# Early blocks of a routed expert layer: a second block's tokens chosen by 0/1 matrices, token lists read in another order, three subtractions on another engine

## The chip, the cores and the metric

The kernel runs on one core of a Trainium2 chip. The metric is the device time of one execution in microseconds, from the runs listed below. A profiled execution records every instruction of the five engines: TensorE (PE in the profile: matmuls and transposes), VectorE (DVE), ScalarE (ACT), GpSimd (POOL) and SyncE (SP, which here only starts DMAs and reads small numbers into its registers). Each engine takes its own instructions strictly in order; an instruction starts when the semaphores that it names have been raised by the engines or DMAs it depends on.

## The reference, cut to what matters

The program computes three layers one after the other: an attention with a feature map, a mixture of 8 experts weighted by a Sinkhorn table ("MoE1"), and a mixture of 8 experts in which every token goes to one expert only ("MoE2"). The change lies at the seam of the second and the third:

```
logits = xn @ en.T / tau                  # 2304 tokens, 8 experts
expert_idx = argmax(logits, axis=1)
gate_w = softmax(logits)[token, expert_idx]
for e in range(8):
    mask = expert_idx == e
    h = max(x[mask] @ w1[e], 0)           # 512 -> 1024
    out[mask] = gate_w[mask] * (h @ w2[e])  # 1024 -> 512
```

All of it is in fp32. Products on TensorE are made of three matmuls on high and low parts (high x high, low x high, high x low), so weights and activations are split into a rounded high part (ScalarE) and the rest (VectorE).

## The kernel before, in words

**MoE1** goes over pairs (expert group n = 0..15, third of the tokens bi), 768 tokens each. At the end of the list stand the thirds 0, 1, 2 of the last group. When a third is done, its 6 tiles of 128 tokens are final rows of x, and are routed while the next third is being multiplied: `route_a` (transposes, row norms, rows to DRAM `x2d`, L896 on), `route_l` (logits), `route_b`/`route_o` (argmax as a 0/1 row), `route_c` (running counts by matmul), `route_s`/`route_d`/`route_w` (softmax weight and slot number of each token), and `route_i` (L988): GpSimd writes (token number, gate weight) of each token by an indirect DMA to its slot in one of the four DRAM tables `ids[0..3]` (tile number modulo 4). A slot is expert x 2304 + rank, so each expert's list lies packed.

**MoE2** goes over 22 static blocks of 128 tokens (`second(0, 22)`). The first 6 (`NEARLY`) hold only tokens of the first two thirds (`NF` = 12 tiles), so they can begin before the last third is routed; the others come from all tokens, after `other_blocks` has made their table. For each block:

- `load_regs` (SP) reads the block's offset, expert and "new expert" flag from the table `meta`; `load_ids` (L1108, SP) reads the block's piece of each of the four tables, four DMAs into `idr`. These wait for every scatter written ahead of them in the program.
- `gather` adds the four pieces (GpSimd for the first blocks, L1115 and L1116), casts the token numbers (L1123), and fetches the rows by an indirect DMA into `xgs` (L1125).
- `tx` (L1191) transposes the rows, and splits them into `xth` (ScalarE) and `xtl` (VectorE). `p1` is 24 matmuls of 128x512 (L1209 to L1211), `relu` (L1219) writes `hr`, `th_` (L1224 to L1228) transposes and splits it into `hTh` and `hTl`, `p2` is 24 matmuls (L1242 to L1244), scaled by the gate weight on ScalarE (`y`, L1249) and scattered to the output (L1250).
- `wcond` (L1157, SP) loads a quarter of the next block's W1 or W2 into `rw`, on the condition that the expert changes; `wsplit` makes the high part (`s1h`, `s2h`: ScalarE, L1182) and the low part (`s1l`, `s2l`: VectorE, L1183). A buffer of `rw` is loaded again when both have read it; the load's semaphore is raised also when the condition is false.

**The order** is written out by hand. `tail` is a table of (tick, function); ticks 0 to 39 lie in the second but last third of MoE1's work, 40 and above in the last one, whose plain part `p2_plain` (ticks 54 to 69) is six 128x384 matmuls to a tick. What follows, up to block 2, is the straight list in `second` under `if i0 == 0`. A function emits its instructions on all its engines at its place, and each engine's queue gets them in that order.

Block 0 is fetched otherwise: `gather_first` compares, for each of 12 tiles, the slot numbers less the block's offset with the row 0..127 (VectorE, L1141), and multiplies the twelve 0/1 matrices so made with the token numbers (12 matmuls of two columns, L1146). This gives its token numbers without `ids`. It is a generator of 8 steps; each step from the second on makes two compares. `load_ids(0)` and `gather(0)` then serve only the gate weight `gt[0]`, and `load_ids(1)`/`gather(1)` give block 1's rows.

Of the kernel before, what the change touches and what calls it, by code (L numbers as in the profile page):

```python
# [44 lines left out]
def build(tc, a, out):  # L45
# [836 lines left out]
    def batch(t0):  # L882
        if t0 not in rt:
            if t0 == TPB:
                pieces = [live["h3"].tile([P, 2 * TH], F32, tag="r" + q_, name=f"rows{t0}{q_}").unsqueeze(1)[:, :, 0:DM] for q_ in "abcd"]
                pieces += [raw().unsqueeze(1)[:, :, 0:DM] for _ in range(2)]
            else:
                pieces = [live["h3"].tile([P, 2, DM], F32, tag=f"hT{k + 2}", name=f"rows{t0}_{k}") for k in range(TPB // 2)]
# [55 lines left out]
    def route_c(t0):  # L944
        r = rt[t0]
        n, oh = r["n"], r["oh"]
        r["pr"] = psum("B" if t0 == TPB else "C", [P, 6, E])
# [95 lines left out]
    def first_blocks():  # L1043
# [19 lines left out]
        V.scalar_tensor_tensor(out=live["slots"][:, NF:NF + 1], in0=ei[:, 0:1], scalar=float(REG), in1=ri[:, 0:1], op0=ALU.mult, op1=ALU.add)  # L1063
# [37 lines left out]
    xgs = []  # L1101
# [8 lines left out]
    def gather(i):  # L1110
        ig = c0.tile([P, 2], F32, tag="gt", bufs=5, name=f"ig{i}")
        r = idr.pop(i)
        eng = G if i < NEARLY else V
        if i < NEARLY:
# [12 lines left out]
    def gather_first():  # L1127
# [19 lines left out]
        ig = live["slots"][:, NF + 1:NF + 2]  # L1147
        V.tensor_reduce(out=ig, in_=ps, axis=AX.X, op=ALU.add)
        idt[0] = c0.tile([P, 1], I32, tag="idt", bufs=5, name="idt0")
        V.tensor_copy(idt[0], ig)  # L1150
        xg[0] = xgs[0][:, 0, :]
        G.indirect_dma_start(out=xg[0], out_offset=None, in_=x2d[0:NF * P, :], in_offset=bass.IndirectOffsetOnAxis(idt[0][:, :1], 0))
# [24 lines left out]
    def wsplit(i, which, c):  # L1177
# [5 lines left out]
        V.tensor_tensor(out=lo, in0=r, in1=f32(hi), op=ALU.subtract)  # L1183
# [86 lines left out]
    def first_w1(i, cs):  # L1270
        for c in cs:
            wsplit(i, 1, c)
            wcond(i + 1, 1, c)

    def first_w2(i, cs):
        for c in cs:
            wsplit(i, 2, c)
# [97 lines left out]
    tail = route_steps(0, (1, 2, 4, 6, 8, 10), (1, 2, 3, 4, 5, 6), b=8, o=9, p=11, c=11, d=13, s=20, w=21, i=(22, 23, 24, 25, 26, 27))  # L1375
    tail += [(k, partial(route_l, TPB, i + 3 * (j // 4), (j % 4,))) for j, k in enumerate((19, 19, 21, 23, 25, 27, 29, 41)) for i in range(3)]
    tail += route_steps(6, (24, 26, 28, 41, 41, 42), (), p=42, b=41, o=41, c=42, d=42, s=56, w=57, i=(58, 58, 59, 60, 61, 62))
    tail += [(k, partial(next, rf, None)) for k in (43, 44, 46, 47, 62)]
    tail += [(k, partial(next, gf, None)) for k in (23, 49, 50, 51, 52, 53, 54, 56)]
    tail += [(48, partial(load_regs, 0)), (56, partial(load_regs, 1))]  # L1380
# [3 lines left out]
    tail += [(63, partial(load_ids, 1)), (63, partial(load_ids, 0)), (67, partial(gather, 1)), (67, partial(gather, 0)), (67, partial(load_ids, 2)), (68, partial(load_ids, 3))]  # L1384
# [61 lines left out]
    def second(i0, i1):  # L1446
        def w1_next(i, cs, hook=no):
            for c in cs:
                wsplit(i + 1, 1, c)
                hook()  # L1450
# [12 lines left out]
        if i0 == 0:  # L1463
            t0 = NA
            p1(0)
            gather(2)
            first_w1(1, (0, 1))
            first_w2(0, (3,))
            relu(0)
            first_w1(1, (2, 3))  # L1470
            load_ids(4)
# [10 lines left out]
            route_p(t0)  # L1482
            route_b(t0)
            route_o(t0)
            first_w1(2, (0,))
# [143 lines left out]
```

## Time and profile before

| | us |
|---|---|
| runs | 1898.66, 1898.28, 4289.9 |
| median | 1898.66 |
| the profiled execution | 1898.09 |
| its span, first to last instruction | 1896.2 |
| TensorE busy in it | 1878.8 (99%) |
| VectorE, ScalarE, GpSimd busy | 1284.2, 861.6, 968.5 |

All times inside the trace count from the start of the span. The last third of MoE1 ends at about 1610; block 0 of MoE2 begins there, and from block 2 on a block takes about 12.4 us. A row of a timeline gives start, duration, engine, line, operation, tiles and shape; in square brackets the idle time ahead of it and what ended that. `xN` folds N like instructions that follow each other.

### The profile page before, as it was taken

What the parts mean: (1) busy time and instruction counts of PE and PEld (TensorE: products, weight loads), DVE (VectorE), ACT (ScalarE), POOL (GpSimd) and SP (SyncE); (2) the same over time, 40 slices, a digit from 0 to 9 for tenths busy, and PEclk for the clock granted to TensorE, in tenths of its full rate; (3) what the DMA queues carried; (4) which work ended last, traced back from release to release, by engine and by line L of the source; (5) the groups of instructions that cost most, each with busy time, mean ns of one, the idle gap of its engine ahead of it and who ended that gap; (6) DMA issues with size and microseconds to landing.
All of it is one profiled execution on the core that took longest, in us unless ns stands there. A gap on an engine that the chain in (4) does not pass through costs nothing.

```text
span 1896.2 us, 34764 instructions
## 1 busy us (share of the span) xinstructions
PE 1878.8 (99%) x13649; PEld 1795.6 (95%) x13649; DVE 1284.2 (68%) x1667; ACT 861.6 (45%) x1258; POOL 968.5 (51%) x687
## 2 busy tenths in 40 slices
PE   9999999999999999999999999999999999999998
PEld 8999999999999999999999999999999998788886
DVE  7775676665756657567566575665656647899995
ACT  5674342433333333424243333333342324889885
POOL 0241377746556564747474655656474733522211
PEclk9999999999999999999999999999999999999999
DMA  5474544536372736354453637272635353263960
GB/s 169 153 277 184 216 153 152 178 125 213 103 244 90 252 86 224 114 189 157 147 178 125 212 103 245 79 263 83 228 114 189 117 181 123 63 224 101 339 207 33
DMA packets 125161, 314.47 MB, mean 166 GB/s; under 512 B 23336, under 2 KB 72248, under 8 KB 124994
## 3 DMA queue, kind: packets, MB, share of 16 engines
q1 hardware_dynamic: 120898, 301.69, 47.2%
q0 software_dynamic: 4096, 10.51, 1.6%
q8 instruction: 110, 1.80, 0.4%
q14 instruction: 57, 0.47, 0.1%
HBM read 335.29 MB, written 32.44 MB: 194 GB/s over the span
## 4 chain that ended last, share of the span: by engine, by line
PE 74%; POOL 14%; issue 6%; DVE 2%; DMA 2%; ACT 1%; POOLq 0%; SPq 0%; DVEq 0%; ACTq 0%
PE Q L414 16%; PE Q L415 15%; PE Q L413 15%; POOL w1S L333 3%; POOL hB L461 3%; POOL hT L461 3%; POOL w1A L333 2%; PE psR L146 2%; PE psA L1210 2%; PE psA L1209 2%; PE psA L1211 2%; PE psD L1244 2%; PE psD L1243 2%; PE psD L1242 2%; PE psD L203 2%
## 5 line engine op out<-in xcount | busy, mean ns | idle before, releaser
L477 DVE TENSOR_TENSOR acca<-acca,Q 128x768 f32<-128x768 f32 x196 | 181.4, 949 | 134.5 <-PE Q L415 134.5
L461 POOL TENSOR_TENSOR hB<-rb,hB 128x768 fp32r<-128x768 f32 x42 | 77.7, 1850 | 181.8 <-ACT hB L458 181.8
L413 PE MATMUL Q<-hT,w2S 128*128 128x384 f32 x504 | 169.9, 337 | 0.1
L415 PE MATMUL Q<-hT,w2S 128*128 128x384 f32 x504 | 168.5, 334 | 0.0
L414 PE MATMUL Q<-hT,w2S 128*128 128x384 f32 x504 | 168.4, 334 | 0.0
L415 PE MATMUL Q<-xT,w1S 128*128 128x384 f32 x504 | 168.3, 334 | 0.0
L413 PE MATMUL Q<-xT,w1S 128*128 128x384 f32 x504 | 168.3, 334 | 0.0
L414 PE MATMUL Q<-xT,w1S 128*128 128x384 f32 x504 | 168.3, 334 | 0.0
L477 DVE TENSOR_TENSOR accb<-accb,Q 128x768 f32<-128x768 f32 x98 | 90.7, 949 | 70.7 <-PE Q L415 70.7
L473 DVE TENSOR_TENSOR Q<-Q,ra 128x768 f32<-128x768 f32 x42 | 40.6, 966 | 132.1 <-PE Q L415 127.6
L333 POOL TENSOR_TENSOR w1A<-raw,w1A 128x512 fp32r<-128x512 f32 x48 | 62.7, 1307 | 131.0 <-ACT w1A L332 131.0
L482 ACT COPY ra<-Q 128x768 f32<-128x768 f32 x42 | 33.7, 801 | 188.0 <-PE Q L415 166.5
L415 PE MATMUL Q<-hB,w2A 128*128 128x384 f32 x338 | 113.0, 334 | 0.0
L413 PE MATMUL Q<-hB,w2A 128*128 128x384 f32 x338 | 112.9, 334 | 0.0
L414 PE MATMUL Q<-hB,w2A 128*128 128x384 f32 x338 | 112.9, 334 | 0.0
L461 POOL TENSOR_TENSOR hT<-ra,hT 128x768 fp32r<-128x768 f32 x42 | 77.5, 1844 | 69.2 <-ACT hT L458 69.2
L413 PE MATMUL Q<-xB,w1A 128*128 128x384 f32 x336 | 112.2, 334 | 0.0
L414 PE MATMUL Q<-xB,w1A 128*128 128x384 f32 x336 | 112.2, 334 | 0.0
L415 PE MATMUL Q<-xB,w1A 128*128 128x384 f32 x336 | 112.2, 334 | 0.0
L1183 DVE TENSOR_TENSOR s1l<-rw,s1h 128x1024 fp32r<-128x1024 f32 x88 | 102.5, 1218 | 4.0 <-ACT s1h L1182 2.4
L473 DVE TENSOR_TENSOR Q<-Q,rc 128x768 f32<-128x768 f32 x42 | 40.6, 966 | 91.6 <-PE Q L415 91.6
L461 POOL TENSOR_TENSOR hT<-rd,hT 128x768 fp32r<-128x768 f32 x42 | 77.7, 1851 | 47.4 <-ACT hT L458 47.4
(477 smaller groups left out, 6124.0 us busy)
## 6 DMA issues: line engine op xcount, KB each, us to landing
xT<-xpd SPq DMA_DIRECT2D x120, 768.0 KB
rw<-in_moe_w SPq DMA_DIRECT2D x176, 512.0 KB
xB<-xpd SPq DMA_DIRECT2D x90, 768.0 KB
raw<-in_moe_w SPq DMA_DIRECT2D x34, 512.0 KB
gate<-gd SPq DMA_DIRECT2D x45, 384.0 KB
rx<-in_moe_w SPq DMA_DIRECT2D x30, 512.0 KB
xpd<-xT SPq DMA_DIRECT2D x12, 768.0 KB
xpd<-xB SPq DMA_DIRECT2D x9, 768.0 KB
```

The lines of the kernel that those rows point to most:

```text
L146: T.matmul(hs[h_][:, c * P:(c + 1) * P], r[rs, c * P:(c + 1) * P], wphi[rs, :], start=True, stop=True)
L203: T.matmul(ps[cs, 2 * ci + h_, :], eq[:, sg, h_, ci * P + cs.start:ci * P + cs.stop], kvz[:, h_, sg, o:o + W], start=(sg == 0), stop=(sg = ...
L333: eng.tensor_tensor(out=t[:, 1], in0=r(nm), in1=f32(t[:, 0]), op=ALU.subtract)
L413: T.matmul(bank, w[:, 0, j, k, :], x[:, 0, k, :], start=start and k == 0, stop=False, skip_group_check=True)
L414: T.matmul(bank, w[:, 0, j, k, :], x[:, 1, k, :], start=False, stop=False, skip_group_check=True)
L415: T.matmul(bank, w[:, 1, j, k, :], x[:, 0, k, :], start=False, stop=stop and k == 1, skip_group_check=True)
L461: eng.tensor_tensor(out=hb[nm][:, 1], in0=src, in1=f32(hb[nm][:, 0]), op=ALU.subtract)
L473: V.tensor_tensor(out=out, in0=x, in1=y, op=op)
L477: V.tensor_tensor(out=z, in0=z, in1=ps, op=op)
L1183: V.tensor_tensor(out=lo, in0=r, in1=f32(hi), op=ALU.subtract)
L1209: T.matmul(ps[hf], th[:, k, :], wh[:, cs], start=(k == 0), stop=False)
L1210: T.matmul(ps[hf], tl[:, k, :], wh[:, cs], start=False, stop=False)
```

## The change

- `gather_first` makes the token numbers of block 1 too, in 15 steps: after block 0 the slot numbers are moved to block 1's offset, and twelve more compares, twelve more matmuls and a second gather follow. The steps stand at ticks 23, 49 to 52, 56, 57, 59 (block 0; before 23, 49 to 54, 56) and 60 to 63, 65, 67, 69 (block 1).
- `load_ids(1)`, `load_ids(0)`, `gather(1)`, `gather(0)` leave the table. The lists of blocks 0 and 1, now wanted for the gate weight alone, are read in `second`: block 0's after block 1's first weights and `gather(0)` behind `route_p`; block 1's ahead of the last third's scatters, and `gather(1)` behind `p2(0)`.
- Block 2's list is read at tick 63 and gathered at 69 (before 67, and behind `p1(0)`), and block 4's where block 5's was.
- `load_ids(5)` stood ahead of `p1(1)`; it now stands behind the six `route_i` of the last third and the two W2 splits after them.
- Block 6's list is read one step later (behind W2 of block 3), and its pieces are added on GpSimd. The steps of `other_blocks` come with every second piece of W1 rather than with each.
- Three low parts are made by GpSimd: the fourth quarter of block 0's W2, and the first two quarters of block 2's W1.
- Some routing steps of the first and second third move by 1 to 15 ticks; the last third's rows have six buffers of one tile rather than three of two, and are written to `x2d` one by one.

```
     def gather(i):
-        eng = G if i < NEARLY else V
-        if i < NEARLY:
+        eng = G if i <= NEARLY else V
+        if i <= NEARLY:
...
     def gather_first():
-        slots, offs = live["slots"][:, 0:NF], live["slots"][:, NF:NF + 1]
-        V.tensor_scalar(out=slots, in0=slots, scalar1=offs, scalar2=None, op0=ALU.subtract)
-        for t in range(NF):
-            V.tensor_scalar(out=oh[:, t, :], in0=iop, scalar1=slots[:, t:t + 1], scalar2=None, op0=ALU.is_equal)
-            if t % 2:
-                yield
-        ps = psum("B", [P, 2])
-        for t in range(NF):
-            T.matmul(ps, oh[:, t, :], idb[:, t, :], start=(t == 0), stop=(t == NF - 1))
...
+        for b in range(2):
+            if b == 0:
+                V.tensor_scalar(out=slots, in0=slots, scalar1=o0, scalar2=None, op0=ALU.subtract)
+            else:
+                V.tensor_scalar(out=slots, in0=slots, scalar1=o0, scalar2=o1, op0=ALU.add, op1=ALU.subtract)
+            for t in range(NF):
+                V.tensor_scalar(out=oh[:, t, :], in0=iop, scalar1=slots[:, t:t + 1], scalar2=None, op0=ALU.is_equal)
+                if t % 2:
+                    yield
+            ps = psum("B", [P, 2])
+            for t in range(NF):
+                T.matmul(ps, oh[:, t, :], idb[:, t, :], start=(t == 0), stop=(t == NF - 1))
...
+            G.indirect_dma_start(out=xg[b], out_offset=None, in_=x2d[0:NF * P, :], in_offset=bass.IndirectOffsetOnAxis(idt[b][:, :1], 0))
+            yield
...
-    tail += [(k, partial(next, gf, None)) for k in (23, 49, 50, 51, 52, 53, 54, 56)]
+    tail += [(k, partial(next, gf, None)) for k in (23, 49, 50, 51, 52, 56, 57, 59)]
...
-    tail += [(63, partial(load_ids, 1)), (63, partial(load_ids, 0)), (67, partial(gather, 1)), (67, partial(gather, 0)), (67, partial(load_ids, 2)), (68, partial(load_ids, 3))]
+    tail += [(k, partial(next, gf, None)) for k in (60, 61, 62, 63, 65, 67, 69)]
+    tail += [(63, partial(load_ids, 2)), (69, partial(gather, 2)), (68, partial(load_ids, 3))]
...
         if i0 == 0:
             t0 = NA
             p1(0)
-            gather(2)
             first_w1(1, (0, 1))
-            first_w2(0, (3,))
+            first_w2(0, (3,), G)
             relu(0)
             first_w1(1, (2, 3))
-            load_ids(4)
+            load_ids(0)
...
             route_p(t0)
+            gather(0)
             route_b(t0)
             route_o(t0)
-            first_w1(2, (0,))
-            load_ids(5)
+            first_w1(2, (0,), G)
+            load_ids(4)
             p1(1)
-            first_w1(2, (1,))
+            first_w1(2, (1,), G)
...
             first_w1(2, (2,))
             tx(2)
             gather(4)
+            load_ids(1)
             for k in range(NTL - NA):
                 route_i(t0, k)
             first_w1(2, (3,))
             first_w2(1, (0, 1))
+            load_ids(5)
             p2(0, 0)
             p2(0, 1)
+            gather(1)
```

On SP, around the list of block 5 (`idr5`) and the quarters of block 2's W2 (`rw2_0` to `rw2_3`; `rw1` is W1). An `ISA` row ahead of each DMA is left out here. Before, block 5's list is read ahead of all these weights:

```order
L1108 DMA idr5_16406<-ids0_83 128x2
L1108 DMA idr5_16406<-ids3_86 128x2
L1157 DMA rw1_1_15730<-in_moe2_w1 128x1024
L1157 DMA rw1_2_15743<-in_moe2_w1 128x1024
L1157 DMA rw1_3_15757<-in_moe2_w1 128x1024
L1157 DMA rw2_0_15771<-in_moe2_w2 128x1024
L1157 DMA rw2_1_15783<-in_moe2_w2 128x1024
L1157 DMA rw2_2_15856<-in_moe2_w2 128x1024
L1157 DMA rw2_3_15858<-in_moe2_w2 128x1024
```

With the change, in the same place (`idr1` is block 1's list):

```order
L1165 DMA rw1_2_15743<-in_moe2_w1 128x1024
L1110 DMA idr1_16486<-ids0_83 128x2
L1110 DMA idr1_16486<-ids3_86 128x2
L1165 DMA rw1_3_15757<-in_moe2_w1 128x1024
L1165 DMA rw2_0_15769<-in_moe2_w2 128x1024
L1165 DMA rw2_1_15779<-in_moe2_w2 128x1024
L1110 DMA idr5_16538<-ids0_83 128x2
L1110 DMA idr5_16538<-ids1_84 128x2
L1110 DMA idr5_16538<-ids3_86 128x2
L1165 DMA rw2_2_15837<-in_moe2_w2 128x1024
L1165 DMA rw2_3_15839<-in_moe2_w2 128x1024
```

Block 5's four reads have moved behind the first half of block 2's W2 and stand ahead of its second half; in the program they now also come behind the last third's scatters into `ids`.

On VectorE, at the last compares (`ohs`) of block 0, ticks 53 to 59 of the last third; `accb` is MoE1's sum of that third, `ss`, `lg`, `se` and `pay` are routing. Before:

```order
L571 TENSOR_TENSOR psA564_15714<-psA564_15714,tu_15660 128x384
L429 SCALAR_TENSOR_TENSOR graw1_15722<-psA564_15714,gate7_2_15325 128x384
L1141 TENSOR_SCALAR ohs_15384<-ohs_15384,slots_3461 128x128 x4
L838 TENSOR_TENSOR accb_2921<-psD565_15773,accb_2921 128x384
L961 TENSOR_SCALAR ss6_15291<-ss6_15291 128x6
```

With the change:

```order
L429 SCALAR_TENSOR_TENSOR graw1_15722<-psA564_15714,gate7_2_15325 128x384
L838 TENSOR_TENSOR accb_2921<-psD565_15771,accb_2921 128x384
L963 TENSOR_SCALAR ss6_15278<-ss6_15278 128x6
L964 RECIPROCAL ss6_15278<-ss6_15278 128x6
L965 TENSOR_TENSOR lg6_15536<-lg6_15536,mxr6_15538 128x48
L1148 TENSOR_SCALAR ohs_15382<-ohs_15382,slots_3461 128x128 x2
L838 TENSOR_TENSOR accb_2921<-psD566_15772,accb_2921 128x384
L984 TENSOR_REDUCE se6_15848<-lg6_15536 128x6
L986 RECIPROCAL pay_127<-se6_15848 128x6
L1148 TENSOR_SCALAR ohs_15382<-ohs_15382,slots_3461 128x128 x2
```

The last two pairs of compares now stand behind two additions into `accb` and the routing of the second third, which they preceded.

On GpSimd, with the change, ahead of the last third's scatters (`L990`):

```order
L1118 TENSOR_TENSOR ig0_15918<-idr0_16244 128x2
L1191 TENSOR_TENSOR s1l2_0_16369<-rw1_0_15728,s1h2_0_16368 128x1024
L1191 TENSOR_TENSOR s1l2_1_16432<-rw1_1_15730,s1h2_1_16431 128x1024
L1117 TENSOR_TENSOR idr4_16400<-idr4_16400 128x4
L1118 TENSOR_TENSOR ig4_16480<-idr4_16400 128x2
L1127 DMA xgs_15381<-x2d_82,idt4_16483 128x512
L990 DMA ids0_83<-pay_127,si12_16457 19456x2
```

Two of the three splits that GpSimd takes over stand in its queue between block 0's list and block 4's, ahead of the scatters.

## Rows read from the trace of the kernel before

**Rows 1.** The page: the span, and the busy time of each engine.
```profile
span 1896.2 us, 34764 instructions
PE 1878.8 (99%) x13649; PEld 1795.6 (95%) x13649; DVE 1284.2 (68%) x1667; ACT 861.6 (45%) x1258; POOL 968.5 (51%) x687
```

**Rows 2.** Waits of TensorE, 1560 to 1900: total, times, longest us.
```profile
PE psA L1191 <- DMA xgs<-x2d,idt: 3.2, 1, 3.2
PE psB L1146 <- DVE ohs L1141: 0.7, 1, 0.7
```

**Rows 3.** Stretches: length, busy us of each engine, PEclk, DMA share, GB/s.
```profile
1620.00:1640.00 20.00, 19.61 (x133) 16.75 (x134) 14.84 (x35) 15.12 (x25) 9.08 (x15) 0.92 0.33 94
1640.00:1660.00 20.00, 20.00 (x97) 16.59 (x97) 19.80 (x31) 19.77 (x25) 10.88 (x8) 1.00 0.05 15
```

**Rows 4.** Timeline of TensorE: start, us, what.
```profile
1591.09 0.66 PE L1146 MATMUL psB<-ohs 128*128 128x2 bf16 x4 [0.74 <-DVE ohs L1141]
...
1620.39 1.08 PE L1191 MATMUL psA<-ident,xgs 128*128 128x128 f32 x4 [3.25 <-DMA xgs<-x2d,idt]
...
1624.37 0.49 PE L1209 MATMUL psA<-s1h,xth 128*128 128x512 f32 x1
...
1654.85 0.60 PE L1191 MATMUL psA<-ident,xgs 128*128 128x128 f32 x4
1655.21 0.48 PE L1242 MATMUL psD<-s2h,hTh 128*128 128x512 f32 x1
```

**Rows 5.** Chain that ended last, in order of time, 1580 to 1625.
```profile
1603.60 6.80 DMA ids<-pay,si
1610.41 2.90 DMA idr<-ids
```

**Rows 6.** Timeline of GpSimd.
```profile
1613.47 0.55 POOL L1115 TENSOR_TENSOR idr<-idr 128x4 f32<-128x4 f32 x1 [8.90 <-DMA idr<-ids]
1614.11 1.05 POOL L1116 TENSOR_TENSOR ig<-idr 128x2 f32<-128x2 f32 x1
...
1622.26 0.20 POOL L1116 TENSOR_TENSOR ig<-idr 128x2 f32<-128x2 f32 x1
...
1638.69 1.00 POOL L988 DMA_INDIRECT ids<-pay,si  x1 [0.91 <-DVE hTl L1228]
...
1647.99 1.29 POOL L988 DMA_INDIRECT ids<-pay,si  x1 [0.30 <-issue]
```

**Rows 7.** Timeline of SP's DMA queue.
```profile
1601.91 12.13 SPq L1108 DMA_DIRECT2D idr<-ids  x8
...
1636.17 1.93 SPq L1108 DMA_DIRECT2D idr<-ids  x4
1638.48 22.17 SPq L1157 DMA_DIRECT2D rw<-in_moe_w  x19
```

**Rows 8.** Instructions on the tile ids, 1636 to 1660: the scatters' time to landing.
```profile
DMA to landing us min/median/max: 4.6/5.6/7.1
```

**Rows 9.** Timeline of ScalarE.
```profile
1645.02 3.93 ACT L1182 CAST s2h<-rw 128x1024 fp32r<-128x1024 f32 x4
1648.82 0.72 ACT L1249 ACTIVATE y<-psD,ig 128x512 f32<-128x512 f32 x1
1649.40 0.62 ACT L1227 CAST hTh<-psD 128x512 fp32r<-128x512 f32 x1
```

**Rows 10.** Timeline of VectorE.
```profile
1590.79 0.73 DVE L1141 TENSOR_SCALAR ohs<-ohs,slots 128x128 bf16<-128x128 bf16 x4
1591.44 0.55 DVE L838 TENSOR_TENSOR accb<-psD,accb 128x384 f32<-128x384 f32 x1
```

**Rows 11.** Costliest groups of the page: busy, mean ns, idle before.
```profile
L461 POOL TENSOR_TENSOR hB<-rb,hB 128x768 fp32r<-128x768 f32 x42 | 77.7, 1850 | 181.8 <-ACT hB L458 181.8
...
L333 POOL TENSOR_TENSOR w1A<-raw,w1A 128x512 fp32r<-128x512 f32 x48 | 62.7, 1307 | 131.0 <-ACT w1A L332 131.0
...
L1183 DVE TENSOR_TENSOR s1l<-rw,s1h 128x1024 fp32r<-128x1024 f32 x88 | 102.5, 1218 | 4.0 <-ACT s1h L1182 2.4
```

More of the change, by code (lines that the diff above doesn't have):

```diff
@@ L886, in batch @@
                 pieces += [raw().unsqueeze(1)[:, :, 0:DM] for _ in range(2)]
+            elif t0 == NA:
+                pieces = [live["h3"].tile([P, 1, DM], F32, tag=t_, name=f"rows{t0}_{t_}") for t_ in ("ra", "rb", "rc", "rd", "hT3", "hT4")]
             else:
@@ L946, in route_c @@
         n, oh = r["n"], r["oh"]
-        r["pr"] = psum("B" if t0 == TPB else "C", [P, 6, E])
+        r["pr"] = psum("B" if t0 < NF else "C", [P, 6, E])
         o = r["pr"][:, 0:n, :].rearrange("p n e -> p (n e)")
@@ L1062, in first_blocks @@
         V.tensor_scalar(out=ri, in0=ri, scalar1=float(P), scalar2=None, op0=ALU.mult)
-        V.scalar_tensor_tensor(out=live["slots"][:, NF:NF + 1], in0=ei[:, 0:1], scalar=float(REG), in1=ri[:, 0:1], op0=ALU.mult, op1=ALU.add)
+        V.scalar_tensor_tensor(out=live["slots"][:, NF:NF + 2], in0=ei[:, 0:2], scalar=float(REG), in1=ri[:, 0:2], op0=ALU.mult, op1=ALU.add)
         yield
@@ L1100, in build @@
     idt, idr, xg, gt = {}, {}, {}, {}
-    xgs = []
+    xgs, igs = [], {}
     def load_ids(i):
@@ L1137, in gather_first @@
         yield
-        slots, offs = live["slots"][:, 0:NF], live["slots"][:, NF:NF + 1]
-        V.tensor_scalar(out=slots, in0=slots, scalar1=offs, scalar2=None, op0=ALU.subtract)
-        for t in range(NF):
-            V.tensor_scalar(out=oh[:, t, :], in0=iop, scalar1=slots[:, t:t + 1], scalar2=None, op0=ALU.is_equal)
-            if t % 2:
-                yield
-        ps = psum("B", [P, 2])
-        for t in range(NF):
-            T.matmul(ps, oh[:, t, :], idb[:, t, :], start=(t == 0), stop=(t == NF - 1))
[L1147 to L1152, printed above, removed]
+        slots = live["slots"][:, 0:NF]
+        o0, o1, ig = (live["slots"][:, NF + i:NF + i + 1] for i in range(3))
+        for b in range(2):
[10 more added lines that the diff above has]
+                T.matmul(ps, oh[:, t, :], idb[:, t, :], start=(t == 0), stop=(t == NF - 1))
+            V.tensor_reduce(out=ig, in_=ps, axis=AX.X, op=ALU.add)
+            idt[b] = c0.tile([P, 1], I32, tag="idt", bufs=5, name=f"idt{b}")
+            igs[b] = c0.tile([P, 2], F32, tag="gt", bufs=5, name=f"ig{b}")
+            V.tensor_copy(idt[b], ig)
+            xg[b] = xgs[0][:, b, :]
+            G.indirect_dma_start(out=xg[b], out_offset=None, in_=x2d[0:NF * P, :], in_offset=bass.IndirectOffsetOnAxis(idt[b][:, :1], 0))
+            yield
     def wcond(i, which, c):
@@ L1175, in places, with wsplit @@
         return [pool.tile([P, 1024], F32R, tag=t_, name=f"s2{q_}{nm}") for q_, (pool, t_) in zip("hl", place)]
-    def wsplit(i, which, c):
+    def wsplit(i, which, c, eng=V):
         r = rw[which][c]
@@ L1182, in wsplit @@
         A.copy(hi, r)
-        V.tensor_tensor(out=lo, in0=r, in1=f32(hi), op=ALU.subtract)
+        eng.tensor_tensor(out=lo, in0=r, in1=f32(hi), op=ALU.subtract)
         w2t[which, i, c] = (hi, lo)
@@ L1449, in w1_next @@
                 wsplit(i + 1, 1, c)
[L1450 removed]
+                if c % 2:
+                    hook()
                 if i + 2 < i1:
@@ L1517, in second @@
             relu(i)
-            if i + 3 == NEARLY:
-                for _ in ob:
-                    pass
-                load_ids(i + 3)
             if i + 1 < i1:
@@ L1532, in second @@
             w2_this(i, partial(next, ob, None))
-            if i + 3 >= NEARLY and i + 3 < i1:
+            if i + 3 == NEARLY:
+                for _ in ob:
+                    pass
+                load_ids(i + 3)
+            elif i + 3 > NEARLY and i + 3 < i1:
                 gather(i + 3)
```

20 lines of the change are left out of this document (10 added, 10 removed).

## The prediction

> **What bounds the kernel now.** I read first the page: TensorE is busy for 1878.8 of the span's 1896.2 us [rows 1], so only its gaps, its clock and its own added work can move the time. The waits of TensorE come second. Around the seam they are few: 3.2 us once at block 1's transposes, for its rows (`xgs`), and 0.7 us once at block 0's 0/1 matmuls, for VectorE's compares [rows 2]. The change can thus win little, and what it puts in TensorE's way may cost more. The stretches come third: in 1640 to 1660 VectorE is busy for 19.80 and ScalarE for 19.77 of 20 us, though TensorE has no gap [rows 3]. Both finish each block's splits just in time there, and neither can make up a delay quickly. In 1620 to 1640 VectorE has 14.84 us, so some 5 us of room [rows 3]. The chain says why block 1 waits: the last scatter of the second third is issued at 1603.60 and lands 6.80 us later, the list's read takes 2.90 us more [rows 5], GpSimd adds and casts, and the gathered rows let TensorE go at 1620.39 [rows 4]. Last comes SP: its eight list reads take 12.13 us from 1601.91 [rows 7], because the first ones stand there until those scatters have landed. Everything behind them on SP stands too; in the kernel before that is nothing urgent.
>
> The sum is made against the profiled execution, 1898.09 us (1.9 us around its span); the median of the runs, 1898.66, lies 0.6 us above it, so the forecast holds for either.
>
> **Part 1: block 1's rows by matrices.** The twelve compares, at 0.73 us for four [rows 10], add 2.2 us to VectorE during the last ticks, where it is not what TensorE waits for. The twelve two-column matmuls add under 1 us to TensorE (the eight ahead of the wait in the kernel before fit into half a microsecond). The gather is issued behind tick 69, near 1611; the chain leaves 1620.39 - 1616.4 = 4 us from the issue of such a gather to TensorE's start, where GpSimd's sum and cast of the list fill 1613.47 to 1616.4 [rows 4, 6], so its rows land near 1615. Block 1's transposes are due at 1617.14, when the 3.25 us wait begins. So the wait goes. What does it give back? Upper bound: from 1617.14 to `p1(1)` at 1624.37 lie 7.2 us [rows 4]; the work in them is four groups of transposes and two of logits, which took 1.08 us a group there and take 0.60 us in a stretch at the full clock (1654.85) [rows 4]. With the wait goes most of that slowness, so at most 5 us. Lower bound 0: ScalarE still has splits, block 0's `hr` and routing rows queued ahead of `xth(1)`. Laying its instructions end to end I get `p1(1)` near 1621, a gain of 3; I take that, nearer the upper bound because VectorE and ScalarE are both under 80% in that stretch [rows 3].
>
> **Part 2: block 0's compares later.** The last pairs stood just ahead of an addition into `accb` of 0.55 us [rows 10]; now two additions and seven routing operations stand ahead of them, while the matmuls moved from tick 57 to 59 only. Laid end to end, VectorE finishes the last pair 1.6 to 2.4 us after TensorE arrives, where it was 0.74 us late [rows 4]. Cost 0.9 to 1.7 us; I take 1. Parts 1 and 2 together give -2, between -4 (all of part 1, little of part 2) and +1.7.
>
> **Part 3: block 5's list behind the scatters.** This decides. In the kernel before, the four reads for block 5 took 1.93 us at 1636.17 and waited for nothing; all of block 1's to 3's weights followed without a stop from 1638.48 [rows 7]. Now the reads are written after the six scatters of the last third, so SP must wait for those to land, and behind SP's wait stand the third and fourth quarter of block 2's W2. That these loads move no data (same expert) doesn't help: `s2h` waits for their semaphore all the same.
>
> - The scatters. They took from 1638.69 to 1647.99, plus 7.1 us at most, 4.6 at least to land [rows 6, 8]. The second third's last one took 6.80 [rows 5]. Their start: block 1's list must be read first, and GpSimd has two splits ahead of them; their slots are known earlier by the 2 us of parts 1 and 2. I take 1638, between 1637 and 1640. The last lands at 1638 + 9.3 + 6.4 = 1653.7; bounds 1637 + 9.3 + 4.6 = 1650.9 and 1640 + 9.3 + 7.1 = 1656.4.
> - SP then issues three more things before the third quarter, at 0.48 us each (1.93 for four [rows 7]): 1.5 us. From there to the start of `s2h`: between 0 and the 2.90 us of a read that carries data [rows 5]; I take 1.3, nearer the lower end, because this load carries none. So the third `s2h` copy begins at 1656.5, where before it was at 1645.02 + 2 x 0.98 = 1647.0 [rows 9]. Bounds 1652.4 and 1660.8.
> - From it to `p2(2)` on TensorE: ScalarE has two copies at 0.98, `y` 0.72 and `hTh` 0.62 [rows 9], 3.3 us; VectorE beside it has two subtractions at 1.22 [rows 11] behind the first copy, small table operations and `hTl`, about 4.5 us. I take 4.5. TensorE, by then idle for 6 to 10 us, resumes slowly: after 3.25 us of idleness the granted clock of that stretch was 0.92 rather than 1.00 [rows 3], 0.08 x 20 = 1.6 us; I take 1.5 again, with bounds 0 and 2.
> - `p2(2)` counted at full clock thus begins at 1656.5 + 4.5 + 1.5 = 1662.5; before 1655.21 [rows 4]. **+7.3 us.** Bounds: 1652.4 + 4.5 = 1656.9 (+1.7), and 1660.8 + 4.5 + 2 = 1667.3 (+12.1).
>
> Parts 1 and 2 don't come on top: TensorE merely comes to this wait 2 us sooner and waits longer. Nor is it won back later, since the blocks after it are paced by TensorE at its own speed.
>
> **Part 4: the rest, at nothing.** GpSimd takes three 128x1024 subtractions. It does not do this shape in the kernel before; 1307 ns for 512 columns and 1850 for 768 [rows 11] go on to 2.4 us, against VectorE's 1.22. VectorE loses 3.7 us of work in a stretch where it has room; block 0's last split is wanted only by `p2(0)`, behind block 1's whole `p1`, 5.6 us after 1624.37 [rows 4]. The last third's rows go to DRAM in six writes instead of three, 3 more issues of some 0.5 us on SP, ahead of loads that aren't urgent at that point. Block 6's list sum on GpSimd replaces one VectorE operation; cover: block 6's rows are wanted some 30 us later than they come. If the table of blocks 6 to 21 comes late because ScalarE and VectorE are held up at 1650, block 6 follows that delay rather than adding to it: 0 to +2, taken as 0.
>
> **Rivals.**
>
> A. *The hold-up is hidden* (chance 0.17). If the scatters start early (their slots come 2 to 3 us sooner) and land in 4.6 us, SP is free near 1651 and the copies are only about 4 us late; ScalarE might find other work and TensorE enough queued (`p1(3)`). For it: TensorE has `p1(3)` of 5.6 us ahead of `p2(2)`. Against it: that work stands ahead of `p2(2)` already in the kernel before, where `hTh(2)` was done at 1650 and `p2(2)` at 1655.21, so the cover is 5 us and the delay of the copies 9.5. Price: parts 1 and 2 alone, 1898.1 - 2 = 1896.1, and 1894.1 by their lower bound. It ends on the other side, not slower than before. It decides if the third quarter's load is through by 1650.
>
> B. *GpSimd and VectorE in each other's way* (0.08). GpSimd's list additions beside VectorE's subtractions took 0.55 and 1.05 us, and 0.20 us when VectorE wasn't at one [rows 6]. If VectorE is in turn stopped for each of GpSimd's three splits, it loses 3 x 2.4 and saves 3 x 1.22, +3.6 us, and about 2 of it passes its 5 us of room and lands on `p1(1)` and `p1(2)`: without a hold-up 1898; with one, the scatters start 2 to 3 us later and the time is 1908. The Trainium skill ("SBUF — State Buffer", section "Who interferes with whom") says that a VectorE instruction with two SBUF inputs contends with a GpSimd instruction that reads SBUF, and that whichever issues first has the shared ports for its whole length; the trace agrees as far as the five-fold addition goes.
>
> C. *The change doesn't do what it says* (0.05): block 1's gather comes late, since its last compares share VectorE with block 0's late ones, and the transposes still wait. Without the hold-up that gives 1898 to 1899, with it nothing changes, since part 3 is counted from the scatters.
>
> **How the numbers follow.** The hold-up as worked out has 0.70: 1898.1 + 7.3 = 1905.4, from 1899.8 to 1910.2. The range goes down to rival A's 1896.1 less a microsecond, and up to the bound of part 3 and a little for a later table: 1895 to 1911. It leaves out some 15 in 100: a gain above 3 us, or a hold-up with a second wait at block 6. A change of over 2% is 38 us, about what a measurement of this kernel can tell from none; no case comes near it. Faster by that 0.01, within 0.97, slower 0.02.
>
> **What would show it.** The wait of 3.2 us for `xgs` at block 1's transposes is gone, `p1(1)` begins near 1621 (part 1). TensorE waits about 2 us for `ohs` before 1595 (part 2). SP's reads for block 5 stand for 10 to 15 us until some 1654; ScalarE's third `s2h` copy of block 2 waits for `rw`, and TensorE then has its largest wait of the seam, 7 to 10 us, at `p2(2)`, with a lowered clock behind it (part 3). From block 3 on the blocks follow at 12.4 us, late by a constant. I am wrong if `p2(2)` begins before 1656, or if TensorE waits longest somewhere else.

## The result, and the profile after

The changed kernel takes 1914.39 us in the median of its runs, against 1899.04 for the kernel before: a ratio of 1.0079 with a 95% interval of [1.0065, 1.0094], or 15 us more (12 to 18). By the 2% bound this is no change; it is slower all the same, and lies above the range that was forecast (1895 to 1911, with 1905.4 as the likeliest). The profiled execution took 1916.35 us, its span 1914.5. One run in each kernel's list, above 4000 us, is a disturbed one: it stands in the two medians (1913.87 and 1898.66 without it) and not in the ratio.

The path of TensorE shows where the time went. These are starts of its work in the two traces, read from its timeline:

| TensorE begins | before | after | difference |
|---|---|---|---|
| `p1(0)` | 1610.17 | 1611.67 | +1.50 |
| `p1(1)` | 1624.37 | 1621.65 | -2.72 |
| `p2(0)` | 1630.54 | 1629.38 | -1.16 |
| `p2(2)` | 1655.21 | 1663.39 | +8.18 |
| `p1(4)` | 1661.57 | 1673.23 | +11.66 |
| transposes of block 6 | 1679.71 | 1694.95 | +15.24 |
| `p1(6)` | 1686.42 | 1704.27 | +17.85 |

From there on the difference stays at 17.85: the blocks after it run at the same 12.3 us. (This profiled execution is 2 us above its kernel's median.)

The waits of TensorE in the changed kernel, 1560 to 1920 (total, times, longest), the answer to [rows 2]:

```profile
PE psD L1250 <- ACT hTh L1235: 8.7, 1, 8.7
PE psA L1199 <- DMA xgs<-x2d,idt: 4.5, 2, 3.7
PE psA L1218 <- DVE xtl L1203: 1.3, 1, 1.3
PE psA L413 <- DVE tu L571: 0.7, 1, 0.7
PE psD L1252 <- DVE hTl L1236: 0.6, 1, 0.6
PE psB L1153 <- DVE ohs L1148: 0.4, 1, 0.4
```

L1250 is block 2's second product, and its 8.7 us are the wait that was forecast. The 3.7 us for `xgs` is no longer block 1's: it is block 6's, a wait that the forecast took at 0 and left out of its range. The product in TensorE's timeline, with both of its waits:

```profile
1663.39 0.80 PE L1250 MATMUL psD<-s2h,hTh 128*128 128x512 f32 x1 [8.74 <-ACT hTh L1235]
...
1665.18 0.80 PE L1252 MATMUL psD<-s2h,hTl 128*128 128x512 f32 x1 [0.56 <-DVE hTl L1236]
```

The stretches (columns as in [rows 3]) show the clock behind both waits:

```profile
1640.00:1660.00 20.00, 14.65 (x72) 11.81 (x70) 11.27 (x18) 5.89 (x8) 11.48 (x10) 0.99 0.10 27
1660.00:1680.00 20.00, 16.05 (x64) 12.69 (x65) 18.39 (x32) 19.50 (x27) 6.24 (x6) 0.76 0.12 41
1680.00:1700.00 20.00, 16.30 (x68) 13.25 (x67) 17.92 (x21) 14.43 (x19) 9.08 (x6) 0.84 0.65 210
```

SP's DMA queue and ScalarE, where [rows 7] and [rows 9] had no stop:

```profile
1631.50 0.09 SPq L1165 DMA_DIRECT2D rw<-in_moe_w  x1
1633.56 1.90 SPq L1110 DMA_DIRECT2D idr<-ids  x4
...
1636.56 1.91 SPq L1110 DMA_DIRECT2D idr<-ids  x4
1638.83 0.93 SPq L1165 DMA_DIRECT2D rw<-in_moe_w  x3
1655.17 4.64 SPq L1110 DMA_DIRECT2D idr<-ids  x4
1660.20 16.89 SPq L1165 DMA_DIRECT2D rw<-in_moe_w  x18
1679.21 5.72 SPq L1110 DMA_DIRECT2D idr<-ids  x8
```

```profile
1643.85 2.05 ACT L1190 CAST s2h<-rw 128x1024 fp32r<-128x1024 f32 x2
1660.29 1.99 ACT L1190 CAST s2h<-rw 128x1024 fp32r<-128x1024 f32 x2 [14.39 <-DMA rw<-in_moe_w]
```

SP issues nothing from 1639.8 to 1655.17, while it stands at block 5's list; W2's third quarter follows at 1660.20, and ScalarE copies it at once, having stood 14.39 us. This is the hold-up as described. GpSimd and VectorE of the same trace:

```profile
1618.18 2.38 POOL L1191 TENSOR_TENSOR s2l<-rw,s2h 128x1024 fp32r<-128x1024 f32 x1
...
1629.08 4.76 POOL L1191 TENSOR_TENSOR s1l<-rw,s1h 128x1024 fp32r<-128x1024 f32 x2
...
1636.97 0.34 POOL L1117 TENSOR_TENSOR idr<-idr 128x4 f32<-128x4 f32 x1 [3.13 <-DMA idr<-ids]
...
1639.86 1.03 POOL L1127 DMA_INDIRECT xgs<-x2d,idt  x1 [0.28 <-POOL idt L1125]
1641.19 2.04 POOL L990 DMA_INDIRECT ids<-pay,si  x1 [0.30 <-DVE nb L1004]
...
1650.91 0.97 POOL L990 DMA_INDIRECT ids<-pay,si  x1 [0.31 <-issue]
...
1684.74 4.89 POOL L1127 DMA_INDIRECT xgs<-x2d,idt  x1 [0.58 <-DVE xtl L1203]
```

```profile
1618.98 3.81 DVE L1191 TENSOR_TENSOR s1l<-rw,s1h 128x1024 fp32r<-128x1024 f32 x2 [2.71 <-ACT s1h L1190]
...
1629.42 2.12 DVE L974 TENSOR_TENSOR sl<-sl,oh 128x48 f32<-128x48 f32 x1
1631.58 0.20 DVE L976 TENSOR_REDUCE sf<-sl 128x6 f32<-128x48 f32 x1
1631.81 2.06 DVE L978 CAST si<-sf 128x6 int32<-128x6 f32 x1
```

A VectorE operation of 128x48 elements takes 2.12 us and ends at 1631.54, as GpSimd's first split (half of 4.76 us from 1629.08) ends at 1631.46; a cast of 6 columns then takes 2.06 and ends at 1633.87, with the second (1633.84). The reduction between them takes its 0.20 us beside the second split. The two weight subtractions at 1618.98 take 3.81 rather than 2.36, beside GpSimd's split of block 0's W2 (1618.18 to 1620.56). So these VectorE operations stand still for what is left of a GpSimd split.

Two of the delayed operations make the last third's slots, but it isn't the slots that the scatters begin with. They are there at 1633.87 and the gate weights at 1634.41; the first scatter begins at 1641.19, right behind the gather of block 4's rows, which stands ahead of it on GpSimd and had to wait for block 4's list. (The 0.30 us ahead of it are no wait for the VectorE operation named there: as much lies ahead of the later scatters.) SP read that list only from 1633.56, behind a weight load at 1631.50, and this load had waited for GpSimd to be through with the same buffer (SP's waits, 1630 to 1700):

```profile
SPq L1165 <- POOL s1l L1191: 3.0, 1, 3.0
```

### The profile page after: what moved, and what is told of

It reads as the page before. It is cut to its first block, busy times and chain, and to the rows that moved or that the text cites. A ratio compares the mean times of both kernels' runs of the same rounds, so it can differ in the third digit from the quotient of the medians.

```text
span 1914.5 us, 34805 instructions
## 1 busy us (share of the span) xinstructions
PE 1884.0 (98%) x13661; PEld 1797.6 (94%) x13661; DVE 1289.7 (67%) x1677; ACT 861.5 (45%) x1258; POOL 978.8 (51%) x692
## 4 chain that ended last, share of the span: by engine, by line
PE 73%; POOL 14%; issue 7%; DMA 3%; DVE 2%; ACT 1%; SPq 0%; POOLq 0%; DVEq 0%; ACTq 0%
PE Q L414 15%; PE Q L415 15%; PE Q L413 15%; POOL w1S L333 3%; POOL hB L461 3%; POOL hT L461 2%; PE psR L146 2%; POOL w1A L333 2%; PE psD L203 2%; PE psA L413 1%; PE psD L413 1%; PE psA L1218 1%; PE psD L1252 1%; PE psA L1219 1%; PE psA L1217 1%
## 5 line engine op out<-in xcount | busy, mean ns | idle before, releaser
L1191 DVE TENSOR_TENSOR s2l<-rw,s2h 128x1024 fp32r<-128x1024 f32 x75 | 88.0, 1219 | 21.5 <-ACT s2h L1190 21.3
```

Source lines behind the costliest of these rows:

```text
L1191: eng.tensor_tensor(out=lo, in0=r, in1=f32(hi), op=ALU.subtract)
```

## The experiments

All ratios are to the kernel before, run beside each on the same chip; one ten-thousandth is 0.19 us. The chips differ: the kernel before had medians of 1898.94 (e1 to e4), 1904.2 (e5 to e8), 1898.63 (e9 to e12), 1902.47 (e13 to e16) and 1902.77 (e17, e18) on the five chips, so no times of whole runs are compared across them. Where a place in a trace is set against the kernel before, that is the first chip's trace.

**e1: block 5's list read ahead of the scatters again**

```
             load_ids(1)
+            load_ids(5)
             for k in range(NTL - NA):
                 route_i(t0, k)
...
             first_w2(1, (0, 1))
-            load_ids(5)
```

> The changed kernel with one call moved: block 5's list is read ahead of the last third's scatters (right behind block 1's list), so its reads wait for nothing. Theory 1 (SP's hold-up causes both of TensorE's large waits, the one at block 2's second product and, through the late table and the late list, the one at block 6's transposes): both go, the second product of block 2 starts near 1654, 1 us before the kernel before; 1896 to 1899 us. Theory 2 (the wait at block 6 is the change's own: its list is read a step later and summed on GpSimd): the first wait goes, the second stays with its slow clock, 4 to 6 us; 1902 to 1905 us. Rival (GpSimd's splits delay the scatters and so everything): 1905 us or more.

Measured 1906.59 us, 1.0044 [1.0027, 1.0061]. Theory 1 in its full form fell: half of the loss is left. TensorE's waits in its trace, 1575 to 1900:

```profile
PE psA L1199 <- DMA xgs<-x2d,idt: 4.8, 3, 2.8
PE psA L1218 <- DVE xtl L1203: 2.9, 2, 2.3
PE psD L1250 <- ACT hTh L1235: 1.3, 1, 1.3
```

The 8.7 us wait is 1.3; the waits for `xgs` stay, the longest at block 6.

**e2: the kernel before, with only that read put late**

```
             first_w1(2, (0,))
-            load_ids(5)
...
             first_w2(1, (0, 1))
+            load_ids(5)
```

> The kernel before with that one call put late: block 5's list is read behind the last third's scatters and the first half of block 2's W2; nothing else of the change. Theory 1: SP stands for over 10 us, the second product of block 2 starts 8 to 12 us late with a slow clock behind it, and block 6's rows come late too: 1910 to 1915 us. Theory 2: the first wait only, block 6 in time: 1908 to 1911 us. If the hold-up were not the cause: 1898 to 1900 us.

Measured 1903.52, 1.0020 [1.0011, 1.0030]: slower, but by 4.6 us where 9 to 16 were expected. In this order the scatters begin at 1637.15, and SP is through at 1654.03 instead of 1660.20, when the work in the trace is already 2 us late for another reason. ScalarE waits 4.9 us for W2's third quarter, but TensorE doesn't wait for `hTh`; it loses 3.0 us up to block 5's transposes, with waits of 0.9 and 1.8 us for VectorE's `hTl` and `xtl`. The hold-up's price depends on when the scatters start.

**e3: block 6's table, list and sum as before**

```
             relu(i)
+            if i + 3 == NEARLY:
+                for _ in ob: pass
+                load_ids(i + 3)
             if i + 1 < i1:
                 tx(i + 1)
...
-        eng = G if i <= NEARLY else V
+        eng = G if i < NEARLY else V
```

(and a step of the table with every piece of W1.)

> The changed kernel, with block 6 as in the kernel before: its table finished by a step with every quarter of W1, its list read a step earlier (ahead of block 3's transposes) and summed on VectorE. Theory 1: the wait at block 2's second product stays, block 6 still waits, perhaps a little less: 1911 to 1915 us. Theory 2: the first wait stays, the second (3.7 us and its slow clock, 6.4 us together) goes: 1907 to 1909 us.

Measured 1908.95, 1.0056 [1.0039, 1.0072]. The wait for block 6's rows is gone, the first wait stays (8.3 us). Theory 2 holds: the second wait is the change's own.

**e4: the three splits back on VectorE** (the argument `, G` taken away three times)

> The changed kernel with its three GpSimd splits back on VectorE. Theories 1 and 2: the scatters begin 0 to 2 us earlier, since two splits (4.8 us) leave GpSimd's queue ahead of them, but the landing decides: 1911 to 1915 us. Rival (the splits hold up the scatters): the scatters begin 3 to 4 us earlier and the waits shrink by as much: 1908 to 1911 us.

Measured 1910.97, 1.0061 [1.0044, 1.0078], at the edge of the rival's range; its interval and the change's overlap, and the pairs below decide. The scatters begin at 1638.00, 3.2 us earlier (1.0 of them is there at `p1(0)` already, 1610.66 against 1611.67). The slots' operation is short again, and SP's weight load and block 4's list come earlier:

```profile
1627.60 0.09 SPq L1165 DMA_DIRECT2D rw<-in_moe_w  x1
1630.25 1.90 SPq L1110 DMA_DIRECT2D idr<-ids  x4
```

```profile
1628.45 0.21 DVE L974 TENSOR_TENSOR sl<-sl,oh 128x48 f32<-128x48 f32 x1
```

From the read of that list to the first scatter it is 1638.00 - 1630.25 = 7.8 us, and 1641.19 - 1633.56 = 7.6 in the change; from the slots being there it is 8.9 and 7.3. The scatters follow the list.

So three things seem to cost. The remaining combinations of the three were run together:

> The changed kernel with both waits taken away: block 5's list ahead of the scatters, and block 6's table, list and sum as in the kernel before; GpSimd keeps its three splits. If the second wait is block 6's late table (theory 2, as its own experiment bore out) and nothing else is left, TensorE is 0.6 us ahead at block 2's second product and stays about there: 1898 to 1901 us. If GpSimd's splits also delay block 5's rows (rival: they hold VectorE at block 1's rows and at the last third's slots, and these the scatters), a wait of 2 us at block 5's transposes remains: 1901 to 1903 us.

> The changed kernel with block 5's list ahead of the scatters and the three splits on VectorE; block 6's table, list and sum stay late. Block 2's second product then starts 3 us ahead of the kernel before. Theory 2: block 6's transposes still wait, 5 to 7 us with the clock: 1900 to 1903 us. Rival (the waits behind block 5 come from GpSimd's splits): 1896 to 1898 us.

> All three undone; what is left of the change is block 1's tokens by matrices, the lists of blocks 0 and 1 read late, and the shifted routing. The gain that block 1's transposes gave, 3.2 us ahead of the kernel before at block 1's second product in the run with splits on VectorE, should now last to the end: 1895 to 1897 us. If something else of the change costs time behind block 2: 1898 to 1901 us.

> The changed kernel with only block 5's list left late; block 6 as before and the splits on VectorE. The hold-up alone, in the changed program: the second product of block 2 starts 4 to 5 us late as in the run with splits on VectorE, the slow clock adds some 2.5, and no second wait follows: 1904 to 1906 us. If the hold-up makes block 6 late by itself: 1908 us or more.

| run | block 5's list | block 6 | splits | ratio |
|---|---|---|---|---|
| the change | late | late | GpSimd | 1.0079 [1.0065, 1.0094] |
| e1 | early | late | GpSimd | 1.0044 [1.0027, 1.0061] |
| e3 | late | old | GpSimd | 1.0056 [1.0039, 1.0072] |
| e4 | late | late | VectorE | 1.0061 [1.0044, 1.0078] |
| e5 | early | old | GpSimd | 1.0007 [0.9998, 1.0017] |
| e6 | early | late | VectorE | 1.0022 [1.0013, 1.0032] |
| e8 | late | old | VectorE | 1.0021 [1.0010, 1.0031] |
| e7 | early | old | VectorE | 0.9990 [0.9980, 1.0000] |

Each part has four pairs that differ in it alone. The late list: 35, 49, 39 and 31 ten-thousandths, 7.3 us in the mean. Block 6: 23, 37, 40 and 32, 6.3 us. The splits: 18, 22, 35 and 17, 4.4 us. A single pair is uncertain by some 20 and the mean of four by some 10, so the order of the three is not sure, but that each of them costs is. Some pairs are taken across chips, ratio against ratio; the three on one chip, e8, e6 and e5 against e7, give 31, 32 and 17. e5 against e7 shows the way of the splits once more: block 4's list is read 1.1 us later (1634.91 against 1633.78), and the scatters begin 1.1 later (1644.24 against 1643.17). What is left, e7, is 1.9 us faster than the kernel before (its interval ends at no difference). The sum, 7.3 + 6.3 + 4.4 - 1.9 = 16 us, is the measured 15 within its interval: the three costs add. The expectations of times were set on the first chip of the experiments; taken as ratios, e5 and e7 came in as their better cases, e6 at the upper edge of theory 2 (1.0022 against 1.0021), and e8 missed: 1.0021, below both of its cases (1.0027 to 1.0037, or more).

In e7 the next wait in line shows, on ScalarE, 1625 to 1675:

```profile
ACT y L1257 <- POOL ig L1118: 6.5, 1, 6.5
```

Block 1's list, now wanted for its gate weight only, is summed on GpSimd behind six scatters; ScalarE waits for it at block 1's output, and block 2's `hTh` stands behind. In the changed kernel SP's hold-up covers this. The sum was put ahead of the scatters, in four kernels (`load_ids(5)` stands there in e9 and e10 only):

```
             load_ids(1)
             load_ids(5)
+            gather(1)
             for k in range(NTL - NA):
...
-            gather(1)
```

> The run with all three undone, and block 1's list sum (gather(1)) moved from behind the second product of block 0 to ahead of the last third's scatters on GpSimd. In that run's trace ScalarE waited 6.5 us for this sum at block 1's output scaling, since six scatters stood ahead of it, and TensorE lost 6 us from block 2's second product to block 5's transposes. If that is the last cost: no wait of ScalarE there, the lead of 1.5 to 3 us at block 2's first product stays to the end, a ratio of 0.9965 to 0.9985 (4 to 7 us below the run without the move). If the loss comes from SP's eight reads in a row instead: no change against that run, ratio 0.999.

> The same, with the compares of block 0 at the ticks of the kernel before (53, 54, 56 in place of 56, 57, 59). In the changed kernel block 0's gather was issued at 1601.27, behind three scatters, and block 0's transposes began 1.1 us late and its first product 1.5 us late. If that is carried on: 0.5 to 1.5 us faster than the run without this. If block 1's compares then only come closer to what VectorE has to do, or the 0.74 us wait at the matmuls of block 0 takes it back: no difference.

> The changed kernel with that move alone. SP's hold-up stands ahead: ScalarE waits for W2's third quarter until 1660 whether or not the sum is there at 1654. So if the two waits cover each other, no change against the changed kernel (ratio 1.006 to 1.008); if they add, 4 us less (1.004 to 1.006).

> The clean run (first of these) with block 5's list late again: the hold-up alone and uncovered. The prediction put it at +7.3 us over the kernel before, and 9 us over a kernel that is 2 us faster; with block 1's sum also costing when not held up, 6 to 7 us was what the full comparison gave. Uncovered it should be 8 to 11 us slower than the clean run.

e9: 1.0013 [1.0004, 1.0022]; e10 (`gather_first` at 53, 54, 56 for 56, 57, 59): 1.0004 [0.9994, 1.0013], some 1.7 us below e9, with intervals that overlap; e11: 1.0095 [1.0079, 1.0110]; e12: 1.0050 [1.0034, 1.0065]. e11, expected at 1.008 at most, is no faster than the change (3 us slower, with intervals that overlap), so the move wins nothing behind the hold-up. e12 against e9 gives the hold-up uncovered, 37 ten-thousandths, 7.0 us: under the 8 to 11 that were expected. e9 itself missed: ScalarE's wait is gone and TensorE keeps 3.36 us of lead up to `p1(4)`, and loses 6.2 at block 5's transposes. GpSimd, at block 5's list:

```profile
1658.71 0.99 POOL L1258 DMA_INDIRECT out<-y,idt  x1 [6.75 <-ACT y L1257]
1659.70 4.42 POOL L1117 TENSOR_TENSOR idr<-idr 128x4 f32<-128x4 f32 x1
```

An addition of four columns takes 4.42 us beside VectorE's subtractions, against 1.01 us in the kernel before at the same step. Then:

```
-            if i + 3 >= NEARLY and i + 3 < i1:
+            if i + 3 >= NEARLY - 1 and i + 3 < i1:
                 gather(i + 3)
```

> The clean run (three parts undone, block 1's sum ahead of the scatters) with block 5's list sums and gather moved one place forward on GpSimd, ahead of the output of block 1. In the clean run's trace TensorE kept 3.36 us of lead up to block 4's first product and lost 6.2 us at block 5's transposes, whose gather stood on GpSimd behind that output (until 1659.7) and behind a list addition that took 4.42 us beside VectorE's subtractions. If that is where the gain goes: no wait at block 5, the lead lasts, ratio 0.997 to 0.999, 5 to 6 us below the clean run. If the next wait (block 6) takes its place: 1.000 to 1.001.

> The same with block 0's compares at the ticks of the kernel before; in the clean pair these gave 0.8 us of lead at block 2. Ratio 0.9965 to 0.9985, about 0.8 us below the run without.

e13: 1.0008 [0.9999, 1.0017]; e14, in whose profiled execution TensorE stood 3.5 us at one run of routing matmuls, waiting for nothing the trace shows: 1.0017 [1.0008, 1.0026]. Neither beats the kernel before, though in e13's profiled execution (span 1896.6) no wait of TensorE at the seam is over 0.8 us. Repeated beside a profile of the kernel before on a further chip:

> The same kernel as e13 once more, beside a profile of the kernel before on the same chip. On the chip of e13 TensorE stood 2.5 us in all at the small routing matmuls (L919), waiting for nothing that the trace shows, which it did not do in the trace of the kernel before. If that comes with the chip, a chip without these stops gives 0.997 to 0.999 here; if it comes with the kernel, 1.000 to 1.002 again, with the stops.

> The kernel before, unchanged, for its profile on this chip. If the stops at the routing matmuls come with the chip, it has them wherever e17 has them, and neither has them elsewhere; if they come with the changed order, only e17 has them. Time as the other runs of the kernel before on this chip.

e17: 0.9997 [0.9988, 1.0006]; e18: 1904.57 us once. TensorE's stops at the routing matmuls come with this chip, since the kernel before has them there too (L917 is L919 of the change), in one piece of 1.2 us. First e17, then e18, over the whole span:

```profile
PE psA L1199 <- DMA xgs<-x2d,idt: 2.7, 1, 2.7
PE psC L919 <- issue: 1.8, 4, 0.5
```

```profile
PE psA L1191 <- DMA xgs<-x2d,idt: 4.8, 1, 4.8
...
PE psC L917 <- issue: 1.2, 1, 1.2
```

So between these two traces they account for no more than 1.8 - 1.2 = 0.6 us. Block 5 waited again in e17, and not in e13, with the same program. The cast of block 5's token numbers on GpSimd, first in e13, then in e17, and VectorE in e17:

```profile
1659.03 0.18 POOL L1125 CAST idt<-ig 128x1 int32<-128x1 f32 x1 [5.52 <-DMA out<-y,idt]
```

```profile
1662.96 4.60 POOL L1125 CAST idt<-ig 128x1 int32<-128x1 f32 x1 [2.90 <-DMA out<-y,idt]
```

```profile
1662.89 1.20 DVE L1191 TENSOR_TENSOR s<-rw,s 128x1024 fp32r<-128x1024 f32 x1
1664.03 3.48 DVE L1191 TENSOR_TENSOR s2l<-rw,s2h 128x1024 fp32r<-128x1024 f32 x3
```

One column per partition: 0.18 us, or 4.60 where VectorE has begun four subtractions 0.07 us earlier (they end at 1667.51, the cast at 1667.56). The Trainium skill ("SBUF — State Buffer", section "Who interferes with whom") says that a VectorE instruction with two SBUF inputs and a GpSimd instruction that reads SBUF contend for one shared pair of ports, held for a whole instruction by whoever came first; here GpSimd waited through four instructions in a row, not one. Which case occurs hangs on fractions of a microsecond. That would fit the spread of e13's eleven runs, 1898.34 to 1906.06, but it isn't shown that each long run has this wait: one run of e13 and one of e17 were profiled.

**e15 and e16: which piece of block 6.** e15 puts back only the place of the read (with the table's drain), e16 only the sum (VectorE).

> The changed kernel with one thing of block 6 as in the kernel before: its table is drained and its list read ahead of block 3's transposes; the sum stays on GpSimd and the table's steps stay at every second piece. If the late read makes the second wait: it goes or falls under 1 us, 1.005 to 1.0065. If the sum on GpSimd does: no change, 1.007 to 1.009.

> The changed kernel with block 6's list summed on VectorE again, the read staying late. If the late read makes the wait: it stays, 1.007 to 1.009. If the sum on GpSimd, which waited 7.7 us for the list and then for its indirect DMA 4.89 us, makes it: 1.005 to 1.0065.

e15: 1.0067 [1.0052, 1.0082]; e16: 1.0074 [1.0059, 1.0089]. The intervals don't separate them from the change. The traces do: TensorE's waits behind 1670, of e15, then of e16:

```profile
PE psA L1199 <- DMA xgs<-x2d,idt: 1.0, 1, 1.0
```

```profile
PE psA L1218 <- DVE xtl L1203: 2.2, 1, 2.2
```

With the early read the wait falls from 3.7 to 1.0 us; with the sum on VectorE it changes its place, since VectorE now stands at the late list ahead of `xtl`. The late read makes most of the wait, and the engine of the sum decides who bears it. By the ratios the two pieces give back 12 and 5 of block 6's 33 ten-thousandths, each uncertain by some 20; the third piece, the table's steps with every second quarter, has no run of its own.

## Why the prediction was right, and where it failed

**Part 1, right.** Block 1's rows are there in time and `p1(1)` began at 1621.65 (near 1621). But 1.3 us of it went at once to a wait for `xtl`, whose place on VectorE is behind the subtractions that GpSimd's split had stretched; with the splits on VectorE (e4) this wait is 0.2.

**Part 2, right in its sum only, and by luck.** TensorE waited 0.4 us for the compares instead of 1.6 to 2.4. What it had wrong is the wait. It also missed a gain: in the kernel before the clock was down behind the compares (`PEclk` 0.83 in 1590 to 1600), in the changed kernel it isn't (1.00). The price came in another place: the gather of block 0 is queued on GpSimd behind three scatters, was issued at 1601.27 instead of 1593.62, and block 0's transposes waited 0.8 us for rows. `p1(0)` was 1.50 late, against 0.9 to 1.7 forecast. Parts 1 and 2 together: -2 forecast, and -1.9 in e7, the kernel that keeps them and drops the three parts. That too is partly luck, since e7 also bears the 6.5 us wait of ScalarE, and e9, without it, isn't faster.

**Part 3, right, with terms off that cancel in part.** The scatters began at 1641.19, outside 1637 to 1640. Without GpSimd's splits they begin at 1638.00, so most of this lateness belongs to part 4. The third `s2h` copy came at 1660.29, against 1656.5 and near its upper bound of 1660.8. From it to `p2(2)` took 3.1 us, not 4.5: the first matmul needs ScalarE's copies alone, the 3.3 us of the same sum, and VectorE's part shows as the 0.6 us for `hTl` further on. Behind the start of `p2(2)` another 11.66 - 8.18 = 3.5 us went, that 0.6 and 2.9 for the slow clock, for which I had taken 1.5: the granted clock was 0.50 from 1663.4 to 1669.5, the first two thirds of the product. I took the term from one case, where it was 0.50 for 2.6 us behind a wait of 3.25 (1620.4 to 1623.0). The length of the wait doesn't tell the loss: behind block 6's 3.7 us the clock was at 0.52 for 5.8 us. The hold-up in itself is 7.3 us in the mean of four pairs and 7.0 uncovered. Against the kernel before I had put it at +7.3, with the early gain already swallowed. The runs show the gain and the hold-up side by side, 7.3 - 1.9 = 5.4; e8, the kernel with the hold-up and neither of the other two, is 4.0 us slower than the kernel before.

**Part 4 failed: "the rest, at nothing".** Two of its terms were mis-sized, and they are the whole miss: 6.3 + 4.4, less the 1.9 by which part 3 was too high, is 8.8, and the miss is 1914.4 - 1905.4 = 9.0.

- Block 6: "0 to +2, taken as 0", because its rows were "wanted some 30 us later than they come". They cost 6.3 us. The 30 us are not in the trace of the kernel before: block 6's list is read at 1662.85, its gather issued at 1667.60, its transposes come at 1679.71 (rows below: SP's queue, GpSimd, TensorE). A gather of this stretch takes 3.4 to 6.3 us to land, which leaves a cover of 6 to 9 us. And the change itself moves the read behind the four splits of block 3's W2 and halves the steps of the table. At nearly the same lateness of `p2(2)` (e3, 1662.53 against 1663.39) the list is read at 1673.23 instead of 1679.21, and the gather issued in 0.97 us rather than 4.89. A step that is moved has to be costed in the order it now has, not in the old one.

```profile
1662.85 2.06 SPq L1108 DMA_DIRECT2D idr<-ids  x4
```

```profile
1667.60 0.96 POOL L1125 DMA_INDIRECT xgs<-x2d,idt  x1 [4.78 <-PE psA L1211]
```

```profile
1679.71 0.60 PE L1191 MATMUL psA<-ident,xgs 128*128 128x128 f32 x4
```

- GpSimd's splits: VectorE "loses 3.7 us of work in a stretch where it has room". They cost 4.4 us. The forecast counted VectorE's room and GpSimd's own queue. It left out who waits for a split: SP's next weight load, block 4's list behind it and the scatters behind that list, which begin 3.2 us later than in e4 (2.2 without what is there at `p1(0)`). VectorE did stand still as well, 1.5 us at the weight subtractions and 1.9 at each of two routing operations, and 1.1 of it reached TensorE at `p1(1)` (1.3 against 0.2 in e4). How the 4.4 us divide between the two is not shown. The standing still is rival B, to which I gave 0.08. Its 1908 with a hold-up had the scatters 2 to 3 us later, which came about, but by another path; and its "about 2 of it passes" doesn't follow from 3.6 us and a room of 5.

The hold-up came together with the splits and with block 6. No case of the forecast held all three, and the second wait at block 6 was left outside the range, which ended at 1911.

**Rival A** (hidden hold-up) did not occur: SP was free at 1660, not 1651. **Rival C** neither: block 1's transposes didn't wait.

**Open.** Why the last 2 to 4 us of the early gain do not reach the end in e13 and e17 in most runs is shown for one profiled execution, not for all. How block 6's cost divides among its three pieces is open as well: two of them are told by waits in the traces only, the third not at all.

## What to carry to other kernels

When one step in a straight list is moved behind writes that it must wait for, look at what stands behind it in its own queue: here loads that move no data, and whose only use was their semaphore. Cost each moved step against the new order, read the cover of a step from its own rows, and give the cases a row in which several of them happen together. VectorE work that was moved to GpSimd was paid for here by whichever engine came second, down to a cast of one column, and by the queue that waited for the slower engine to let a buffer go.

## What the runs showed of the hardware that was not expected

- GpSimd's split of 128x1024 took 2.38 us, as the rows of smaller ones led on (2.4). During it VectorE operations of 0.21 and 0.17 us took 2.12 and 2.06. The other way round a GpSimd cast of one column took 4.60 instead of 0.18.
- After 8.7 us of waiting TensorE lost 2.9 us more to the clock; after 3.7 us, 17.85 - 15.24 = 2.6 us.
- In the traces from three of the five chips of the experiments TensorE stopped at runs of matmuls with 8 columns for 0.5 to 3.5 us at a time, "issue" in the trace, on one of them in e17 and in the kernel before alike; the traces from the two others don't have it. On those two the kernel before was 3.5 to 5.6 us faster.
